# A packed attention with a gated convolution on one core: another hand-written order of issue for all five engines

## The chip, the core and the metric

The kernel runs on one core of a Trainium2 chip. Its engines are PE (TensorE: matrix products, with PEld for its weight loads), DVE (VectorE), ACT (ScalarE), POOL (GpSimd) and SP (SyncE, which here only issues DMA transfers). The metric is the time of one execution on the device in microseconds (us), as the median of several; shorter is better.

## The reference, cut to what matters

Eight batches of eight heads. In each head 32 packed queries `p` attend to 576 keys and values; the 32 results then serve as keys and values for the 576 real queries. The heads are laid side by side (512 columns), and a causal convolution of five taps over the 576 positions gives a gate for a value product, which an output product follows.

```python
def sm_attn(qq, kk, vv):
    s = scale * np.matmul(qq, kk.transpose(0, 1, 3, 2))
    s = s - np.max(s, axis=-1, keepdims=True)
    a = np.exp(s)
    a = a / (np.sum(a, axis=-1, keepdims=True) + 1e-09)
    return np.matmul(a, vv)
p_packed = sm_attn(p, k, v)              # 32 x 64 a head
out = sm_attn(q, p_packed, p_packed)     # 576 x 64 a head
...
for k in range(K):                       # K = 5
    gate_pre += conv_w[k][None, None, :] * xp[:, k:k + S, :]
gate = 1.0 / (1.0 + np.exp(-gate_pre))
val = x @ w_val
return (gate * val @ w_out).astype(np.float32)
```

## The kernel before, in words

The work is cut by batch into nineteen kinds of *streams*, Python generators that issue a few instructions and yield. A letter names the kind and a digit the batch, so `a3.2` means: take two more steps of batch 3's packed attention. The table `ORDER` at the top of the file lists such tokens one after the other, and `run` walks it. The class `InOrder` ties each instruction to the one before it on its engine, so each engine, and SP with its transfers, issues exactly in the order in which the table reaches it, and an instruction that has to wait holds up all that stands behind it on that engine. Tiles come from pools with few buffers (`NB`, `PSB`), and a load into a buffer waits until the last reader of its earlier content is done.

The streams that matter below:

- `K`, `V`, `Q`, `P`: loads of keys, values, queries (two transfers of 576 KB for a batch and tensor) and packed queries (four transfers of 64 KB for two batches), into `km`, `vm`, `qm`, `p`. `L`: loads of the weights (512 KB each), `wv_words` and `wo_words`, with `cw_words` between them.
- `W`, `C`, `O`: the weights come as 64-bit words and are turned into 32-bit numbers by ACT, DVE and POOL. `C` also spreads the convolution weights over the partitions with 40 small products (`spread`), which ACT copies into `cwb`.
- `k`, `q`: DVE transposes into `pT`, `kT` (two halves), `qT` (two halves).
- `a`: packed attention. Scores `s` (called `s1` here), row maximum `nb` on DVE, exponential `a` on ACT, then for each of two groups the transposes `at`, their copy `a1t` on ACT, the product with the values `pv`, and its two scaled copies into `ppd` on ACT.
- `p`: `ppTt`, the turned `ppd`, copied to `ppT` by ACT.
- `s`: scores of the real queries (also named `s`, called `s2` here), then transpose `t` and maximum `mx` on DVE, subtraction on POOL, exponential on ACT. `t`: sum `rs`, scaling on POOL, transpose `a` on DVE, split into high and low parts `a2h`, `a2l`.
- `w`: value weights folded with the packed result, `wp`, split into `wph` (ACT) and `wpl` (DVE).
- `x`: for batches 0 to 2 the convolution is folded into a product of 80 short matmuls for each half of the positions, with the weights `kx` (POOL, from `ppd` and `cwb`); for batches 3 to 7 it is a plain product, and `g` does the five taps on DVE.
- `v` (value product: `val`, then the gate on DVE, `gvh` on ACT, `gvl` on POOL) and `o` (output product `o`, copied by ACT to `osb` and stored).

On PE the groups `s`, `at`, `pv`, `x`, `wp` consist of many short matmuls (32 to 96 rows or columns); the groups `val` and `o` of twelve long ones (128 x 288 and 128 x 512). PSUM gives three two-bank buffers (`big`) for `s` (two each), `at`, `wp`, `x` (two each) and `val`, and one bank each for `pv`/`ppTt` and for `o`. All instructions are recorded under one line of the file, L84 before and L83 in the changed kernel (its table is one line shorter), so rows of the profile are told apart by their tiles.

Of the kernel before, what the change touches and what calls it, by code (L numbers as in the profile page):

```python
# [47 lines left out]
ON_POOL = {'al': (0, 1, 2), 'gvl': (0, 1, 2, 3, 4, 5, 6, 7)}  # L48

ORDER = """  # L50
L0 K0 W0.3 P0 K0 W0.2 L0 P0 W0.3 k0.3 W0.4 L0 a0 K1 W0.2 V0 W0.4 L0 W0.2 K1 a0.2 W0 a0.3 W0 a0 L0 k1 a0 C0.2 W0 k1
a0.2 k1 C0 a0.3 C0 W0.2 V0 a1 C0 W0 C0 a0 Q0 a1 q0 a0 Q0 q0 a1 W0 a0 L0 a1 p0 C0 p0 s0 O0.2 W0 a1 s0.6 P2 t0 P2 V1 C0
O0 a1 s0 C0.2 | V1 C0 a1.2 t0 a1 Q1 t0 s0 t0 a1.2 x0 t0 a1 w0 a1 t0 w0 t0 a1 k2 O0 t0.2 O0.3 Q1 K2 k2 a1 x0 K2 O0 w0
k2 a1 O0 x0 L0 t0 O0 x0 q1 O0 p1 x0 O0 x0 a2 O0.3 q1 a2 O0 x0 p1 a2.2 k3 V2 L0 v0.2 a2.2 K3 v0 a2 O0 K3 a2 s1 x1 a2 k3
O0 s1 a2 v0.2 s1.3 a2 s1.2 v0 t1 s1 t1 v0 k3 v0 a2 v0 a2 v0 V2 a2 t1 O0.2 a3 a2 s1 t1.3 v0 t1 a3 a2 P4 v0.2 a3.2 v0 t1
a3 p2 a3 O0 V3 a3 L0 a3 v0 w1 O0 w1 p2 P4 O0 V3 w1 v0 x1 O0.3 x1 Q2 x1 O0 t1 a3.3 t1 a3.2 q2 x1 K4 O0 a3 O0 v1 x1.2 Q2
k4 q2 O0.3 s2 v1 O0 Q3 O0 v1 a3 K4 O0 s2 v1.2 O0 s2 v1 q3 k4 o0 a3 Q3 s2 v1 s2 V4 s2 o0 s2 v1 Q4 t2 v1.2 s2 K5 v1 k4
t2 s2 o0 t2.5 v1 o0.2 v1 q3 a4 p3 a4.2 o0 K5 o0 v1 a4 p3 s3 o0 t2.2 o0 s3 x2 v1 a4 s3.4 o0.2 v1 a4.2 k5 x2 a4 t2 s3 a4
x2.2 a4 q4 w2.2 k5.2 x2 t3 a4 Q4 P6 w2 v2 P6 s3.2 t3 x2 K6 o0 t3 x2 v2 t3 a5 a4 t3 a4 V4 a5 x3 t3 o1 a5.2 K6 a4 a5 t3
v2 o1 a4 t3 a5 x3 t3 v2 k6 x3 V5 x3 v2 q4 a4 x3 t3 x3 p4 g3 o1 v2.2 k6 p4 v2 x3 Q5 V5 v2 g3 k6 o1 a5.2 v2 o1 g3.3 s4  # L60
v2 s4 a5 v2 K7 s4 o1 g3 q5 s4 g3 v2.2 a5 Q5 s4.2 g3 a5 s4 o1 a5 g3 t4 a5 a6 s4 w3 g3 a5 a6 o1 w3 a5 o1.2 a5 a6 v2 q5
g3 t4 w3 V6 g3 p5 Q6 g3 s4 t4 a6 v3 o1 g3 v3 o1 p5 t4 o1 a6 k7 v3 g3 v2 v3 s5 t4.2 g3 s5 o1 g3 s5 g3.2 t4 v3 s5 t4 s5
o1 t4 v3.2 o2 g3 s5 v3 o2 v3 g3 v3 o2 v3 g3.2 x4.4 o2 k7 x4 o2 v3 a6 x4 s5 q6 g4 a6 o2 g4 a6 g3 o2 Q6 x4 v3 g4 V6 a6
g4 t4 w4 s5 g4 o2 t5 a6 g4 v3 w4 a6.2 g4 w4 g4.3 o2 K7 o2 t5 a6 v4 o2 s5 v3 V7 g4 t5 g4.2 v4 t5 v3 o3 g4 t5 v4.2 t5.2
a6 o3 v4 a6 g4 v4 g4 v4 o3 a6 v4 g4 t5 q6 g4.2 Q7 g4.2 o2 v4 g4 v4 g4 o3 p6 x5.2 k7 o3 p6 t5 o3 x5 o3 v4 s6 o3 s6 g4
o3 x5 o3 s6 x5 s6.2 x5.2 o3 v4 s6.2 t5 v4 q7 a7 t6 o3 v4 s6 a7 g5 o3 g5 Q7 v4 a7 t6 a7 s6 t6 g5 a7 v4 o3 a7.2 w5 g5 a7
w5 g5.2 a7 t6 V7 g5 a7.3 w5 t6 a7 o3 g5.2 o4 a7 g5 a7 g5 v5 q7 a7 o4 v5 p7 g5 o4 g5 v5.2 o4 v5 g5.2 t6 g5 p7 v5.2 t6
v5 g5 o4 t6 v5 g5 s7 g5 v5 g5 o4 g5 s7 g5 t6 s7 o4 v5 o4 g5 x6 s7 x6.2 v5 x6 o4.2 g5 o4 s7.2 x6 t6 v5 x6 w6 t7 v5 g6.2
v5 x6 v5 w6 t7 g6 o5 g6 s7.2 g6 o5 g6 w6 o4 g6 t7 o5 s7 g6 o5.2 t7 o5 v6 g6 o5 g6 t7 g6.3 o5 v6 t7 v6.3 g6 t7 g6 v6 o5
v6.2 g6 o5 v6 o5 g6 t7 g6 v6 o5 g6.2 o5 v6 g6 o5 g6.2 x7.3 v6.2 g6 w7 v6 x7.2 t7.2 v6 w7 x7 v6 g7 o6 w7 o5 g7 o6 g7.3  # L70
o6 g7 v7.2 g7 o6 g7.2 o6 g7.2 v7 o6 x7 g7.2 v7 g7.2 v7.4 g7 o6.2 g7.3 v7.2 g7.4 v7.3 o7 g7 o7.2 v7.3 o7.2 o6 o7.14
o6.3
"""


# [632 lines left out]
```

## Time and profile before

| | |
|---|---|
| median of 3 runs | 288.07 us (287.93 to 290.36) |
| the profiled execution | 288.72 us, of which the profile's span is 286.9 us |
| PE busy | 257.1 us of the span (90%), 3676 matmuls |
| DVE busy | 236.1 us (82%) |
| ACT, POOL busy | 164.6 us (57%), 132.3 us (46%) |
| data | 33.57 MB read, 9.44 MB written |

Busy times are sums over an engine's own instructions; PE's ends are modelled. "PEclk" in the profile is the share of PE's full clock that was granted, in tenths. A wait that the profile can't put down to another engine or a transfer is called "issue". The chain of waits goes back from the last instruction to what released it, step by step.

### The profile page before, as it was taken

How to read it: one execution, taken by the hardware profiler on the slowest of the kernel's cores; microseconds unless marked ns; L12 is line 12 of the kernel's file. 1: busy time of each engine (PE TensorE's matmuls, PEld its weight loads, DVE VectorE, ACT ScalarE, POOL GpSimd, SP SyncE). 2: the span in 40 equal slices, each digit the busy share in tenths (PEclk: the TensorE clock that was granted, in tenths of full speed). 3: DMA queues.
4: the chain of work that ended last, by engine and by line, in shares of the span. 5: the costliest groups of instructions: out<-in, count | busy, mean ns of one | idle time of the engine just before them, and what ended most of it. 6: DMA issues, size and time to landing. Idle time of an engine off the chain costs nothing.

```text
span 286.9 us, 8501 instructions
## 1 busy us (share of the span) xinstructions
PE 257.1 (90%) x3676; PEld 191.0 (67%) x3676; DVE 236.1 (82%) x313; ACT 164.6 (57%) x306; POOL 132.3 (46%) x118
## 2 busy tenths in 40 slices
PE   0545789979899999999999999999999999999994
PEld 0143456667678766777677778766886688687863
DVE  2989489859969887899999989999998999787720
ACT  3372467729863558755847675758755465752421
POOL 1544286838778772324554317254074417401520
PEclk9997559979999999999999999999999999999999
DMA  7999953956594558783620664117111111110114
GB/s 264 318 318 292 329 206 89 279 135 181 204 324 131 197 158 220 198 238 125 200 79 37 203 202 121 73 59 220 39 39 53 57 39 73 40 53 21 39 43 177
DMA packets 25839, 43.56 MB, mean 152 GB/s; under 512 B 5829, under 2 KB 11973, under 8 KB 25802
## 3 DMA queue, kind: packets, MB, share of 16 engines
q1 hardware_dynamic: 25802, 43.02, 48.5%
q8 instruction: 29, 0.48, 0.7%
q14 instruction: 8, 0.07, 0.1%
HBM read 33.57 MB, written 9.44 MB: 150 GB/s over the span
## 4 chain that ended last, share of the span: by engine, by line
PE 66%; DVE 18%; ACT 6%; issue 4%; DMA 2%; POOL 1%; SPq 1%; ACTq 0%; DVEq 0%
PE o L84 26%; PE val L84 13%; DVE sig L84 10%; PE s L84 8%; PE x L84 7%; PE pv L84 5%; PE at L84 4%; DMA wv_words<-in_moe_w_val_dram 2%; PE wp L84 2%; ACT sig L84 1%; PE ppTt L84 1%; ACT a L84 1%; SPq L84 1%; PE spread L84 1%; DVE a2l L84 1%
## 5 line engine op out<-in xcount | busy, mean ns | idle before, releaser
L84 POOL TENSOR_TENSOR gvl<-sig,gvh 128x576 fp32r<-128x576 f32 x32 | 51.3, 1604 | 64.7 <-ACT gvh L84 64.5
L84 DVE SCALAR_TENSOR_TENSOR sig<-xp,cw,sig 128x576 f32<-128x576 f32 x80 | 71.1, 888 | 3.2 <-ACT sig L84 1.8
L84 PE MATMUL o<-woh,gvh 128*128 128x512 f32 x144 | 58.9, 409 | 2.3 <-ACT osb L84 1.6
L84 PE MATMUL o<-woh,gvl 128*128 128x512 f32 x144 | 56.9, 395 | 0.0
L84 PE MATMUL o<-wol,gvh 128*128 128x512 f32 x144 | 56.7, 394 | 0.0
L84 PE MATMUL val<-a2h,wph 128*128 128x288 f32 x128 | 39.9, 312 | 0.0
L84 PE MATMUL val<-a2h,wpl 128*128 128x288 f32 x128 | 38.5, 301 | 0.0
L84 PE MATMUL val<-a2l,wph 128*128 128x288 f32 x128 | 38.2, 299 | 0.0
L84 PEld LDWEIGHTS o<-woh,gvh 128*128 128x128 f32 x144 | 27.0, 188 | 13.7 <-ACT osb L84 3.6
L84 ACT CAST gvh<-sig 128x576 fp32r<-128x576 f32 x32 | 21.6, 674 | 25.3 <-DVE sig L84 25.2
L84 DVE SCALAR_TENSOR_TENSOR sig<-sig,val 128x576 f32<-128x576 f32 x32 | 23.7, 740 | 10.5 <-PE val L84 7.0
L84 PEld LDWEIGHTS o<-woh,gvl 128*128 128x128 f32 x144 | 27.1, 188 | 6.8 <-POOL gvl L84 0.5
L84 ACT ACTIVATE osb<-o 128x512 f32<-128x512 f32 x34 | 20.3, 596 | 17.8 <-PE o L84 14.8
L84 PEld LDWEIGHTS o<-wol,gvh 128*128 128x128 f32 x144 | 27.1, 188 | 5.0
L84 POOL TENSOR_TENSOR t<-t,mx 128x576 f32<-128x576 f32 x16 | 20.1, 1254 | 21.8 <-DVE mx L84 21.8
L84 POOL TENSOR_TENSOR t<-t,rs 128x576 f32<-128x576 f32 x16 | 21.9, 1368 | 17.4 <-DVE rs L84 17.3
L84 PEld LDWEIGHTS val<-a2h,wph 128*128 128x128 f32 x128 | 24.6, 192 | 5.2 <-issue 2.0
L84 PEld LDWEIGHTS val<-a2h,wpl 128*128 128x128 f32 x128 | 24.6, 192 | 0.8 <-DVE wpl L84 0.3
L84 PEld LDWEIGHTS val<-a2l,wph 128*128 128x128 f32 x128 | 24.6, 192 | 0.0
L84 ACT ACTIVATE sig<-sig 128x576 f32<-128x576 f32 x20 | 13.7, 685 | 19.0 <-DVE sig L84 18.9
L84 PE MATMUL s<-kT,pT 32*32 32x288 f32 x512 | 16.0, 461 | 9.5 <-DVE kT L84 9.3
L84 PEld LDWEIGHTS pv<-vm,a1t 96*32 96x32 f32 x768 | 13.3, 119 | 13.9 <-issue 6.1
(80 smaller groups left out, 455.6 us busy)
## 6 DMA issues: line engine op xcount, KB each, us to landing
km<-in_k_dram SPq DMA_DIRECT2D x16, 576.0 KB, 5.9
vm<-in_v_dram SPq DMA_DIRECT2D x16, 576.0 KB, 6.9
qm<-in_q_dram SPq DMA_DIRECT2D x16, 576.0 KB, 6.8
out_dram<-osb SPq DMA_DIRECT2D x36, 256.0 KB, 2.1
wv_words<-in_moe_w_val_dram SPq DMA_DIRECT2D x4, 512.0 KB, 6.1
wo_words<-in_moe_w_out_dram SPq DMA_DIRECT2D x4, 512.0 KB, 8.3
p<-in_p_dram SPq DMA_DIRECT2D x16, 64.0 KB, 4.1
cw_words<-in_moe_conv_w_dram SPq DMA_DIRECT2D x1, 20.0 KB
```

The lines of the kernel that those rows point to most:

```text
L84: made = getattr(self.engine, op)(*args, **kw)
```

## The change

Only the string `ORDER` differs: the same tokens in another sequence, so the same instructions, tiles and transfers, in another order on each engine. No size, buffer count or operation changes. Nearly every line of the table is different; the start reads:

```diff
-L0 K0 W0.3 P0 K0 W0.2 L0 P0 W0.3 k0.3 W0.4 L0 a0 K1 W0.2 V0 W0.4 L0 W0.2 K1 a0.2 W0 a0.3 W0 a0 L0 k1 a0 C0.2 W0 k1
...
+L0 W0.6 L0 K0 W0 P0 K0 W0.2 P0 k0.3 W0.4 a0 L0 V0 a0 W0.3 k1 W0.3 L0 W0.2 L0 W0 a0.2 K1 k1 a0.4 W0 a0 C0 a0 W0 a0.2 C0
...
```

**PE.** The groups of matmuls stand in the same order in both kernels from the first instruction up to and with the scores `s2` of batch 2 (the 39th group), and again from the third value group of batch 5 to the end. Between them, groups move by one to five places. The place where most moves: from the first value group of batch 1 (`val_0`) to the fourth output group of batches 0 and 1 (`o_3`). One row, the first, stands for each group; `s_2` is `s2` of batch 2, `s_4` is `s1` of batch 4, `s_3` is `s2` of batch 3, `ppTt` is that of batch 3. Before:

```order
L84 MATMUL val_0_1258<-a2h_892,wph_1073 128x288
L84 MATMUL s_2_0_1287<-qT_0_1184,ppT_1076 32x288 x2
L84 MATMUL val_1_1333<-a2h_892,wph_1073 128x288
L84 MATMUL o_0_1353<-woh,gvh 128x512
L84 MATMUL val_2_1387<-a2h_892,wph_1073 128x288
L84 MATMUL o_1_1417<-woh,gvh 128x512
L84 MATMUL val_3_1432<-a2h_892,wph_1073 128x288
L84 MATMUL s_4_0_1448<-kT_0_1351,pT_1277 32x288 x2
L84 MATMUL ppTt_1482<-ident,ppd_1044 128x128 x3
L84 MATMUL o_2_1493<-woh,gvh 128x512
L84 MATMUL s_3_0_1514<-qT_0_1349,ppT_1509 32x288 x2
L84 MATMUL o_3_1563<-woh,gvh 128x512
```

In the changed kernel:

```order
L83 MATMUL val_0_1263<-a2h_912,wph_1073 128x288
L83 MATMUL s_2_0_1286<-qT_0_1132,ppT_1035 32x288 x2
L83 MATMUL ppTt_1345<-ident,ppd_1046 128x128 x3
L83 MATMUL val_1_1351<-a2h_912,wph_1073 128x288
L83 MATMUL o_0_1364<-woh,gvh 128x512
L83 MATMUL s_4_0_1387<-kT_0_1329,pT_1327 32x288 x2
L83 MATMUL o_1_1427<-woh,gvh 128x512
L83 MATMUL val_2_1464<-a2h_912,wph_1073 128x288
L83 MATMUL o_2_1482<-woh,gvh 128x512
L83 MATMUL s_3_0_1500<-qT_0_1440,ppT_1442 32x288 x2
L83 MATMUL val_3_1551<-a2h_912,wph_1073 128x288
L83 MATMUL o_3_1568<-woh,gvh 128x512
```

`s_4` now stands ahead of `o_1`, `val_2` and `val_3`, so two value or output groups stand between `s_2` and `s_4` where five stood, and three between `s_4` and `s_3` where one stood; `ppTt` of batch 3 goes five groups ahead. Further on the same is done on a smaller scale: an output and a value group come between the transposes and the `pv` of batch 4, and in batch 7 two value groups come ahead of the second `pv`.

**ACT, from the second `pv` of batch 0 to the first `ppd` of batch 1.** `a_1_0` and `a_1_1` are batch 1's exponentials, `t_0` batch 0's, `ppd` the copies after `pv`. Before:

```order
L84 ACTIVATE ppd_178<-pv_1_292,sm_0_113 128x64
L84 ACTIVATE a_1_0_328,sm_1_254<-s_1_0_255,nb_1_0_319 128x576
L84 ACTIVATE ppd_178<-pv_1_292,sm_0_113 128x2x64
L84 COPY ppT_341<-ppTt_336 128x384
L84 ACTIVATE wo_top<-wo_words 128x512
L84 ACTIVATE wo_words<-wo_words 128x512
L84 ACTIVATE a_1_1_384,sm_1_254<-s_1_1_256,nb_1_1_334 128x576
L84 ACTIVATE t_0_343<-t_0_343 128x18x32
L84 ACTIVATE p_392<-p_392 128x512
L84 COPY cwb<-spread 128x640
L84 COPY a1t_0_467<-at_0_468 96x768
L84 ACTIVATE t_0_343<-t_0_343 128x18x32
```

In the changed kernel:

```order
L83 ACTIVATE ppd_182<-pv_1_289,sm_0_112 128x64
L83 ACTIVATE ppd_182<-pv_1_289,sm_0_112 128x2x64
L83 ACTIVATE a_1_0_334,sm_1_253<-s_1_0_254,nb_1_0_324 128x576
L83 COPY ppT_342<-ppTt_328 128x384
L83 ACTIVATE a_1_1_381,sm_1_253<-s_1_1_255,nb_1_1_340 128x576
L83 ACTIVATE wo_top<-wo_words 128x512
L83 ACTIVATE t_0_344<-t_0_344 128x18x32
L83 ACTIVATE wo_words<-wo_words 128x512
L83 COPY a1t_0_455<-at_0_456 96x768
L83 ACTIVATE t_0_344<-t_0_344 128x18x32
L83 COPY cwb<-spread 128x640
L83 ACTIVATE ppd_454<-pv_0_480,sm_1_253 128x64
```

Both copies into `ppd` now come ahead of the exponential `a_1_0`, and the copy into `cwb` now stands behind the copy `a1t_0` and the second exponential of `t_0`; the scaling of `p` has left this stretch.

**SP, the loads of batches 2 to 4.** Both pieces begin with `vm_0` of batch 2. `km_0` and `km_1` are batch 3's, the first `vm_1` is batch 2's, the second `vm_0` and `vm_1` batch 3's, `qm` is batch 2's; `wo_words` are the third and the fourth quarter of the output weights. Before:

```order
L84 DMA vm_0_756<-in_v_dram 96x4x384
L84 DMA wo_words<-in_moe_w_out_dram 128x1024
L84 DMA km_0_778<-in_k_dram 128x2x576
L84 DMA km_1_797<-in_k_dram 128x2x576
L84 DMA vm_1_931<-in_v_dram 96x4x384
L84 DMA p_1008<-in_p_dram 32x8x64 x4
L84 DMA vm_0_1042<-in_v_dram 96x4x384
L84 DMA wo_words<-in_moe_w_out_dram 128x1024
L84 DMA vm_1_1080<-in_v_dram 96x4x384
L84 DMA qm_0_1135<-in_q_dram 128x2x576
```

In the changed kernel:

```order
L83 DMA vm_0_749<-in_v_dram 96x4x384
L83 DMA km_0_776<-in_k_dram 128x2x576
L83 DMA wo_words<-in_moe_w_out_dram 128x1024
L83 DMA vm_1_885<-in_v_dram 96x4x384
L83 DMA km_1_907<-in_k_dram 128x2x576
L83 DMA wo_words<-in_moe_w_out_dram 128x1024
L83 DMA p_1041<-in_p_dram 32x8x64 x4
L83 DMA qm_0_1078<-in_q_dram 128x2x576
L83 DMA vm_0_1081<-in_v_dram 96x4x384
L83 DMA qm_1_1084<-in_q_dram 128x2x576
```

`km_0` has moved ahead of the third `wo_words`, `km_1` behind `vm_1`; the four transfers of `p` now come behind the fourth `wo_words`, and both halves of batch 2's `qm` have come forward, ahead of batch 3's values.

**DVE, ahead of `wpl` of batch 1.** The first step on the fourth pair of output weights (`wo_words`, one TENSOR_SCALAR) now stands directly behind the maxima `nb` of batch 3, where before it stood three steps ahead of `wpl`, behind the transpose `a` of batch 1. The transpose `a` itself now stands behind `sm` of batch 3. The second step (SCALAR_TENSOR_TENSOR) stands where it stood.

More of the change, by code (lines that the diff above doesn't have):

```diff
@@ L50 @@
 ORDER = """
-L0 K0 W0.3 P0 K0 W0.2 L0 P0 W0.3 k0.3 W0.4 L0 a0 K1 W0.2 V0 W0.4 L0 W0.2 K1 a0.2 W0 a0.3 W0 a0 L0 k1 a0 C0.2 W0 k1
[L52 to L70, printed above, removed]
@@ L71 @@
-o6 g7 v7.2 g7 o6 g7.2 o6 g7.2 v7 o6 x7 g7.2 v7 g7.2 v7.4 g7 o6.2 g7.3 v7.2 g7.4 v7.3 o7 g7 o7.2 v7.3 o7.2 o6 o7.14
-o6.3
+L0 W0.6 L0 K0 W0 P0 K0 W0.2 P0 k0.3 W0.4 a0 L0 V0 a0 W0.3 k1 W0.3 L0 W0.2 L0 W0 a0.2 K1 k1 a0.4 W0 a0 C0 a0 W0 a0.2 C0
+K1 a0 k1 C0 V0 C0 a1 W0 a0.2 C0 W0 Q0.2 a0 q0 a1 q0 p0 W0.2 a1 L0 C0.2 a1 p0 s0 a1 O0 C0 s0 C0 s0.5 a1 O0 s0 C0 | t0
+a1.2 t0 P2 s0 C0 V1 a1.3 O0 x0 L0 t0.4 a1 t0 a1 w0 V1 w0 O0 t0 P2 O0 K2 a1 O0.2 k2 a1.2 w0 x0 k2 O0 Q1 K2 Q1 x0 p1
+x0.2 t0 k2 q1 O0 q1 x1 O0.2 t0 x0.2 p1 O0.4 a2 V2 O0 a2.2 v0 a2 k3 a2 v0 K3 a2.3 s1 O0.2 a2 v0 k3 s1 a2 v0 s1 L0 s1 a2
@@ new lines @@
+s1 v0 V2 s1.2 v0 s1 a2 O0 K3 v0 t1 a2 O0 s1 t1 L0 v0 k3 v0.2 a2 t1.3 a2.2 t1 a3.2 v0 a3 t1 a3 v0 a3 O0 v0 p2.2 v0 a3
+t1 P4 a3 O0 a3 v0 w1.2 O0 w1 Q2 v0 V3 O0 Q2 x1 q2 O0.2 a3 x1 a3 x1 a3.3 t1 P4 x1 q2 O0.2 t1 O0 V3 x1 a3.2 v1 O0.2 K4
+x1 O0 s2 K4 v1 O0.2 a3 O0 k4.2 O0 Q3 s2.2 K5 k4 s2.2 v1 s2 v1 p3 Q3 v1 o0 t2 o0 v1 a4 o0 a4.2 v1 o0 q3 p3 o0 V4 q3 o0
+t2 v1 s2 Q4 t2 s2 t2 a4 t2 a4 v1.2 s2 v1 k5 o0 t2 s3 P6 o0 a4 v1 t2 K5 s3 x2 t2 v1 P6 v1 o0 v1 o0 s3.2 t2 s3 a4 s3 o0
+a4 v1 x2 V4 k5 x2.2 k5 a4 t2 a4 q4 w2.2 s3 K6 x2.2 t3 x2 w2 v2 s3 a4 v2 s3 Q4 a5 t3.3 a5 t3 a4 o1 t3 a5.2 t3 x3 k6 a4
@@ new lines @@
+a5 o1 k6 v2 t3 v2.2 K6 v2 a4 v2 x3 V5 v2 x3 v2 x3 o1 k6 x3 a4 t3 o0 V5 o1 v2 x3 a4 a5 q4 g3.2 x3 p4 g3 p4 g3 t3 g3 o1
+a5.2 Q5 s4 v2 g3 s4 q5 a5 Q5 a5.2 g3 s4 o1 a5 g3 K7 v2 s4 V6 v2.2 o1 s4 v2 a5 s4 w3.2 g3 a5 s4 o1 a5 g3 t4 a5 g3 s4
+g3.2 w3 a6 p5 o1 a6 t4.2 a6 t4 p5 a6 o1 v2 v3 g3 s4 g3 o1 a6 g3 q5 o1 v3 o1 v3.2 s5 g3.2 t4.2 g3 v3 g3 t4 o1 s5 V6 o1
+v3.3 o2 t4 s5.2 o2 s5.2 g3 v3.3 g3.2 x4.2 o2 x4 Q6 o2 k7 x4.2 s5 o2 x4 o2 k7 a6 v3 g3 g4 q6 s5 g4 t4 Q7 a6 o2 g4 t4 x4
+g4.2 v3 a6 o2 g4 w4 v3 g4 t5 o2 w4 g4 t5 a6.3 w4 a6.2 o2 a6 g4.2 v4 o2 g4 t5 v3 o2 s5 v3 g4 v4 o3 Q6 t5.2 a6 g4 a6 v4
@@ new lines @@
+K7 g4 o3 v4 g4 t5 g4 v4.2 t5 g4 v4 g4 v4 t5 g4 v4 q6 o3 g4.2 v4 o3 g4.2 p6 x5 t5 o3 x5.2 o3.2 p6 V7 k7 o3 s6.2 o3 v4
+g4 x5 v4 s6 o3 s6 x5 s6.2 x5 v4 x5 q7 t5 t6 o3 g5 a7 t6 v4 s6 v4 a7.3 v4 o3 a7 t6 g5 Q7 o3 a7 o3 g5 a7 w5 a7 w5 g5 t6
+g5 V7 g5.2 a7.3 w5 t6 g5.2 s6 a7 g5 o4 g5 a7 q7 o4 g5 v5.2 g5 v5 g5 o3 v5 o4 v5 s6 a7.2 o4 g5 t6 a7 g5 v5 p7.2 v5 o4
+t6 v5 g5.2 t6 v5 o4 g5 s7 v5 g5 o4 g5 t6 s7 g5 v5 g5 x6 o4 x6 s7 x6.2 s7.2 o4 s7.2 o4 x6 g5 x6 s7 o4 v5 t6 v5 w6 g6 t7
+v5.3 w6 g6.2 t7 o4 g6 o5 g6 x6 t7 w6 o5 g6 o5.2 g6 t7 g6.2 t7 v6 s7 o5.3 g6.4 v6 o5 v6 o5 t7 v6 g6 t7 g6 v6 o5 v6.3
@@ L73 @@
+g6.2 v6 o5 t7 g6.2 v6 g6 t7 g6 o5.2 g6.2 v6 x7.2 v6 o5 x7 t7 g6 v6.2 w7 x7 o5 v6 w7.2 x7 v6 x7 g7.2 o6 g7.3 o6.2 g7 v7
+o6 g7 o6 v7 g7 x7 v7 g7.3 v7 g7.3 v7 g7 o6.2 v7.2 o6 g7 v7 g7.2 v7 g7 v7 g7.4 v7 o6 v7 g7 v7.2 o7.3 v7.2 o7.16 o6.3
 """
```

## The prediction

> **What bounds the kernel now.** I read the slices first, then a table of stretches, then PE's waits.
>
> ```profile
> span 286.9 us, 8501 instructions
> PE 257.1 (90%) x3676; PEld 191.0 (67%) x3676; DVE 236.1 (82%) x313; ACT 164.6 (57%) x306; POOL 132.3 (46%) x118
> PEclk9997559979999999999999999999999999999999
> DMA  7999953956594558783620664117111111110114
> ```
>
> A slice is 7.2 us. PE's granted clock falls to half in the fourth to sixth and dips again in the ninth; the transfers are at their limit in nearly the first six slices, and are light from the 25th on. The table by stretch (busy time and count for PE, PEld, DVE, ACT, POOL, then PE's clock, DMA share, GB/s) says where PE could still gain:
>
> ```profile
> 25.50:42.60 17.10, 12.44 (x266) 8.01 (x265) 11.55 (x19) 8.86 (x18) 9.13 (x9) 0.50 0.85 253
> 59.70:63.10 3.40, 3.40 (x31) 3.13 (x19) 0.76 (x2) 1.15 (x3) 1.71 (x2) 0.50 0.47 113
> 63.10:80.00 16.90, 16.02 (x401) 11.97 (x399) 15.70 (x22) 14.24 (x29) 12.63 (x10) 1.00 0.67 200
> 80.00:187.00 107.00, 107.00 (x1597) 81.21 (x1593) 95.54 (x129) 66.05 (x127) 50.59 (x48) 1.00 0.55 166
> ```
>
> From 80 to 187 us PE is busy in 107.00 of 107.00 us at full clock. Nothing is to be had there, however the groups are spaced, unless PE's own work shrinks, and that is the same 3676 matmuls. What PE loses, it loses ahead of 80 us, and after 223 us, where DVE leads. So a new order gains by what it does to the first 80 us, and loses by any wait that it brings into the full stretch. PE's waits up to 80 us (total, times, longest) that are not the mere start-up:
>
> ```profile
> PE pv L84 <- issue: 3.7, 2, 2.0
> PE spread L84 <- issue: 1.5, 1, 1.5
> PE at L84 <- DVE wpl L84: 0.9, 1, 0.9
> ```
>
> Three stops of 5.2 us are put down to nothing but "issue". I take them for PE waiting for its own program:
>
> ```profile
> q8 instruction: 29, 0.48, 0.7%
> q8 instruction: 1, 0.02, 5.6%
> 59.13 1.04 PE L84 MATMUL pv<-vm,a1t 96*32 96x64 f32 x43 [1.69 <-issue]
> ```
>
> The first row is the whole span: 29 fetches in 0.48 MB, 16.5 KB each, for 3676 matmuls and as many weight loads: one fetch for about 253 instructions, or 127 matmuls. The second is the window from 56.4 to 57.8 us alone: one fetch lies there, none in the 4.9 us ahead, and `pv` of batch 2 stops after five of its 48 matmuls until 59.13. So a fetch that starts about 56.5 serves PE by 59.1. Why it starts late, SP's issues show:
>
> ```profile
> 47.83 0.34 SPq L84 DMA_DIRECT2D wo_words<-in_moe_w_out_dram  x1
> 48.27 2.43 SPq L84 DMA_DIRECT2D km<-in_k_dram  x2
> 50.79 0.42 SPq L84 DMA_DIRECT2D vm<-in_v_dram  x1
> ```
>
> These four transfers are 512 and three times 576 KB, 2.3 MB, and the fetch begins when they are through. I read it as a queue: the fetch stands behind the loads issued ahead of its request. The Trainium skill (Runtime: NRT & Kernel Launch, "Instruction fetch mechanics") has programs refilled in blocks of 256 instructions, ahead of time and "mostly hidden"; the count agrees, and 26 of the 29 fetches cost PE no marked stop, but three did. By that rule alone this wait could not change, and the third term below would be 0.
>
> **The change part by part.** PE's order is the same through the first 39 groups, up to `s2` of batch 2, which ends at 84.3 us in this trace. All three stops lie ahead of that and fall on the same matmuls as now. The spacing itself, on PE, therefore touches only the full stretch and is worth 0 there by the row of 107.00. What can act early are the other engines' new orders. The sum is made against the profiled execution, 288.72 us.
>
> *Term 1, the start of batch 0 and `cwb`: +0.25 us.*
>
> ```profile
> 27.07 0.73 ACT L84 ACTIVATE a<-s,nb 128x576 f32<-128x576 f32 x1
> 37.02 0.69 ACT L84 COPY cwb<-spread 128x640 f32<-128x640 f32 x1 [0.71 <-PE spread L84]
> 38.60 0.68 ACT L84 ACTIVATE t<-t 128x576 f32<-128x576 f32 x1
> 38.16 1.54 POOL L84 TENSOR_TENSOR kx<-ppd,cwb 128x640 f32<-128x640 f32 x1
> 43.66 2.55 PE x L84 x67
> 104.92 2.59 PE x L84 x80
> ```
>
> ACT's exponential `a` no longer stands between the two `ppd` copies: `ppTt` and `s2` of batch 0 come 0.7 us sooner. But `cwb` now follows the second exponential of `t`, which ends at 39.28: it starts 39.3 - 0.7 = 38.6, ends 39.3, and `kx` starts there instead of at 38.16, 1.1 us late. POOL's next steps and DVE's last transpose follow `kx` in order and release `x` of batch 0, so `x` starts 1.1 us late. It has something to give back: now its first half takes 3.40 us (43.66 to 47.06), with a break after 67 matmuls, against 2.59 for the same 80 at 104.92, 0.8 us. Starting later, its block of program has come. 1.1 - 0.8 = +0.25, rounded; bounds -0.5 (the 0.7 kept) and +1.2 (nothing given back).
>
> *Term 2, `wpl` of batch 1: -0.9 us.*
>
> ```profile
> L84 DVE TENSOR_SCALAR wo_words<-wo_words 128x512 uint32<-128x512 uint32 x4 | 2.3, 586 | 0.5 <-ACT wo_top L84 0.5
> 77.21 2.97 PE x L84 x79
> ```
>
> One `wo_words` step of 0.59 us leaves the way to `wpl`, for which PE waits 0.9 us: -0.6. The `x` behind it takes 2.97 against 2.59, 0.4 us that I count as a fetch just late; in the new order three loads stand ahead of it instead of four (`qm` of batch 2 has gone forward), so 0.3 comes back. Bounds 0 and -1.3, the whole of both.
>
> *Term 3, the stop at 57.4 us: -1.5 us.*
>
> ```profile
> 60.17 3.12 PE val L84 x12
> 64.04 1.78 PE val L84 x12
> ```
>
> `km` of batch 3 now goes ahead of `wo_words` and no longer waits for its buffer; it waits only for DVE's `kT` of batch 2. So 576 KB of the 2.3 MB can pass up to 1.4 us sooner (at the 0.4 MB in a us that the busy slices carry), and the fetch with it. The stop of 1.69 falls to something between 0.3 and 1.69; I take 0.9, a gain of 0.8. The stop also costs clock: the stretch at 0.50 follows it, and twelve `val` take 3.12 us in it against 1.78, 1.34 us. The 0.9 us wait at 76 us brought no fall of the clock, 1.69 did; a stop of 0.9 is on the edge, and I count half, 0.7. Bounds 0 and -3.0, both gone. The skill's page on the clock (TensorE: Matmul & The Clock Gate, "What's actually happening") asks for an idle window of about 3.4 us before the clock falls; by that the 1.34 would not hang on this stop and the term would be -0.8. Here 1.69 us of idle were enough, so the row decides.
>
> *Term 4, new meetings in the full stretch: +0.9 us.*
>
> ```profile
> L84 DVE STREAM_TRANSPOSE kT<-km 128x1152 f32<-128x1152 f32 x16 | 21.4, 1351 | 0.0
> L84 DVE STREAM_TRANSPOSE t<-s 128x576 f32<-128x576 f32 x16 | 12.4, 773 | 7.4 <-PE s L84 7.4
> L84 DVE TENSOR_REDUCE mx<-t 128x18 f32<-128x576 f32 x16 | 11.9, 747 | 0.3
> 82.77 1.54 PE s L84 x63
> 84.31 1.79 PE val L84 x12
> 86.10 2.80 PE o L84 x12
> ```
>
> `s1` of batch 4 now comes right behind `ppTt`, one `val` and one `o`: at 84.31 + 0.3 + 1.8 + 2.8 = 89.2. Its PSUM buffers come free and its keys are there when DVE has done, after `s2` of batch 2 (84.31) at the soonest, with `kT` still at work: one `kT` started beforehand and ending some 0.9 us into it, then `t`, `mx`, the other `kT`, `t`: 84.31 + 0.9 + 0.77 + 0.75 + 1.35 + 0.77 = 88.9. That just meets. DVE is busy in 95.54 of the 107 us, so it has little to catch up with. There are some three such places (also `ppTt` of batch 5, moved ahead by two groups, and the output groups behind it, whose buffer ACT now empties after three more steps). For each the nearest row is the 0.9 us wait for `wpl`; I take 0.3 each, bounds 0 and +2.
>
> After 210 us PE's order is the same again, and DVE, which leads there, has the same work ahead of each `val`: 0, within 0.5 either way.
>
> **The sum:** 0.25 - 0.9 - 1.5 + 0.9 = -1.25, 288.72 to 287.5 for an execution like the profiled one. That one lies 0.65 above the median of the runs, so 288.07 - 1.25 = **286.8 us**. With these terms' own doubts 285.3 to 288.8.
>
> **The rivals.** *A, the program comes in time throughout.* Both the stop at 57.4 and the clock it costs go (-3.0), term 2 goes whole (-1.3), the middle costs nothing: 288.07 - 4.3 = 283.8. For it: the 2.3 MB are the only load ahead of that fetch. Against it: `kT` now stands behind `wpl` on DVE, so `km` may start later than I take it.
>
> *B, slower: the same stop, moved into the full stretch.* From `at` of batch 4 to `at` behind `s1` of batch 5 PE has over 300 short matmuls, almost in one piece in both orders, and needs a fetch in the middle:
>
> ```profile
> q8 instruction: 1, 0.02, 4.9%
> ```
>
> This is the window 108.3 to 109.5 us. It has come in time. In the new order `qm` of batch 4 and both halves of `km` of batch 6 are issued ahead of it, where before the first half of `km` was the only one: two more transfers, 2.9 us at the same rate. If less than about 0.4 us of slack is there now, PE stops. The price is that of the stop at 57.4, 1.69 + 1.34 = 3.0, with the gains of terms 2 and 3 at a third (-0.8) and the middle at its +0.9: 288.07 + 0.25 + 3.0 + 0.9 - 0.8 = 291.4. Against it: that fetch has spare time that no row shows, and other loads have been spread out.
>
> *C, nothing moves.* The loads shift by as much as the requests, the three stops stay: 288.1.
>
> **How the numbers follow.** A measurement of this kernel tells about 1% from no change, 2.9 us. The forecast has a chance of 0.32, C 0.15, A 0.30, B 0.23. A lies beyond the 1%, B just beyond, the forecast and C within. So faster 0.30, same 0.47, slower 0.23. The range reaches towards A and B as far as the bounds go: the lower ends add to -0.5 - 1.3 - 3.0 = -4.8 and the upper to +3.2; I cut both a little, 283.6 to 291.2.
>
> **What would show it.** Right: the "issue" stops at `pv` of batch 0 and at `spread` stay near 2 and 1.5 us; that at `pv` of batch 2 is under 1 us; `x` of batch 0 starts later; the stretch from 80 to 187 us is full but for waits under 1 us. A shows in no half clock after 45 us. B shows in an "issue" stop and half clock between 105 and 120 us. The forecast is wrong if the stretch from 80 to 187 loses over 2 us to ACT or DVE, or if the start up to 40 us moves by over 1 us: nothing above counts on that.

## The result, and the profile after

The changed kernel takes 291.69 us in the median (290.33 to 293.07, six runs) beside 288.0 us of the kernel before on the same chip: a ratio of 1.0143, with an interval of 1.0108 to 1.0177. Ratios, here and below, are taken from the runs within 1.5% of the fastest of their kernel. It is slower by 3.7 us and lies half a microsecond above the predicted range. Its profiled execution took 290.33 us, the shortest of the six, and that of before 288.72, a long one of its kernel; so the two traces differ by 1.6 us where the medians differ by 3.7.

The slices of the changed kernel's page:

```profile
span 288.6 us, 8500 instructions
PE 257.0 (89%) x3676; PEld 190.8 (66%) x3676; DVE 235.7 (82%) x313; ACT 164.1 (57%) x306; POOL 131.7 (46%) x118
PEclk9999558999999999999999999999999999999999
DMA  7999973979617888088143516238101011100014
```

PE has the same work (257.0 and 257.1 us). The half clock comes half a slice later and its second dip is gone. The full stretch, by stretches (PE, PEld, DVE, ACT, POOL, PE's clock, DMA share, GB/s):

```profile
80.00:187.00 107.00, 105.87 (x1541) 80.45 (x1530) 94.56 (x128) 63.67 (x122) 50.34 (x44) 1.00 0.50 153
112.00:114.10 2.10, 1.11 (x17) 0.24 (x12) 0.24 (x1) 0.00 (x0) 0.00 (x0) 1.00 1.01 224
```

PE is no longer busy all of it. 1.13 of the 107 us are lost, and 0.99 of those lie in the two microseconds of the second row, in which the transfers are at their limit and DVE, ACT and POOL have next to nothing to do. PE's waits, first two rows of before that the prediction doesn't show, then those of the changed kernel (total, times, longest):

```profile
PE s L84 <- DVE kT L84: 9.3, 1, 9.3
PE ppTt L84 <- ACT ppd L84: 1.4, 1, 1.4
```

```profile
PE s L83 <- DVE kT L83: 12.4, 1, 12.4
PE pv L83 <- issue: 2.4, 2, 1.2
PE spread L83 <- issue: 1.8, 1, 1.8
PE x L83 <- issue: 1.6, 2, 1.0
PE ppTt L83 <- ACT ppd L83: 0.7, 1, 0.7
PE at L83 <- DVE wpl L83: 0.3, 1, 0.3
```

Two rows are clearly worse. The first scores start at 12.45 us instead of 9.29, so 3.2 us are lost before PE has done anything. And `x`, which had no marked stop, now has two for nothing but "issue". Three rows are better, in the direction forecast: the stops of `pv` (3.7 before), the wait for `ppd` (1.4) and that for `wpl` (0.9). Of the 1.3 us that `pv` gains, 0.8 are in batch 0, where the prediction expected no change. In these two traces PE is 3.2 us late at the first scores, 2.1 at the first `val` of batch 0 (55.01 against 52.93), 0.5 early at the `at` behind `wpl` (75.92 against 76.39) and 0.5 late at `s2` of batch 2 (83.29 against 82.77). So by 83 us this one execution had made most of its late start good.

Where the first 3.2 us go stands in the first rows of SP and ACT (start, duration). Before, then changed:

```profile
0.74 0.36 SPq L84 DMA_DIRECT2D wv_words<-in_moe_w_val_dram  x1
1.63 1.94 SPq L84 DMA_DIRECT2D p<-in_p_dram  x4
6.87 0.63 ACT L84 ACTIVATE p<-p 128x512 f32<-128x512 f32 x1 [1.61 <-DMA p<-in_p_dram]
```

```profile
0.74 0.85 SPq L83 DMA_DIRECT2D wv_words<-in_moe_w_val_dram  x2
2.11 2.06 SPq L83 DMA_DIRECT2D p<-in_p_dram  x4
10.03 0.63 ACT L83 ACTIVATE p<-p 128x512 f32<-128x512 f32 x1 [3.40 <-DMA p<-in_p_dram]
```

The first change of the table, `L0 W0.6 L0 K0` for `L0 K0 W0.3`, puts a second 512 KB of weights ahead of batch 0's keys and packed queries. SP issues `p` half a microsecond later; its data come 3.2 us later, and ACT, DVE's transposes and PE follow. The stop in `x` of batch 2 in the chain of the changed kernel, and the loads that SP issued ahead of it:

```profile
109.86 2.57 PE x L83 x68
112.43 0.99 issue
113.42 0.73 PE x L83 x12
```

```profile
105.34 0.37 SPq L83 DMA_DIRECT2D km<-in_k_dram  x1
105.76 0.46 SPq L83 DMA_DIRECT2D qm<-in_q_dram  x1
106.60 0.37 SPq L83 DMA_DIRECT2D km<-in_k_dram  x1
108.90 0.33 SPq L83 DMA_DIRECT2D vm<-in_v_dram  x1
```

The queues in the window 107.0 to 110.9 us, then in 110.9 to 112.0:

```profile
q1 hardware_dynamic: 624, 1.37, 95.3%
...
q1 hardware_dynamic: 216, 0.42, 98.7%
q8 instruction: 1, 0.02, 5.7%
```

In the first window only data move, 1.37 MB of them with the queues 95% full; PE's program block is read in the second. In the trace of before that fetch lay in the window that begins at 108.3.

### The profile page after: what moved, and what is told of

The parts are those of the page before. It is cut to its first block, busy times and chain, and to the rows that moved or that the text cites. A ratio compares the mean times of both kernels' runs of the same rounds, so it can differ in the third digit from the quotient of the medians.

```text
span 288.6 us, 8500 instructions
## 1 busy us (share of the span) xinstructions
PE 257.0 (89%) x3676; PEld 190.8 (66%) x3676; DVE 235.7 (82%) x313; ACT 164.1 (57%) x306; POOL 131.7 (46%) x118
## 4 chain that ended last, share of the span: by engine, by line
PE 66%; DVE 20%; ACT 5%; issue 4%; DMA 2%; SPq 1%; POOL 1%; ACTq 0%; DVEq 0%
PE o L83 26%; DVE sig L83 13%; PE val L83 11%; PE s L83 9%; PE x L83 7%; PE pv L83 5%; PE at L83 3%; PE wp L83 2%; DMA p<-in_p_dram 2%; ACT sig L83 2%; DVE rs L83 1%; PE ppTt L83 1%; SPq L83 1%; PE spread L83 1%; DVE kT L83 1%
## 5 line engine op out<-in xcount | busy, mean ns | idle before, releaser
L83 POOL TENSOR_TENSOR gvl<-sig,gvh 128x576 fp32r<-128x576 f32 x32 | 49.9, 1561 | 66.7 <-ACT gvh L83 64.7
L83 DVE SCALAR_TENSOR_TENSOR sig<-xp,cw,sig 128x576 f32<-128x576 f32 x80 | 72.6, 907 | 3.1 <-ACT sig L83 1.6
L83 PE MATMUL val<-a2h,wph 128*128 128x288 f32 x128 | 39.2, 306 | 0.0
L83 PE MATMUL val<-a2h,wpl 128*128 128x288 f32 x128 | 37.9, 296 | 0.2 <-DVE wpl L83 0.2
L83 PEld LDWEIGHTS val<-a2h,wph 128*128 128x128 f32 x128 | 24.0, 188 | 5.0 <-issue 1.3
```

The lines of the kernel that those rows point to most:

```text
L83: made = getattr(self.engine, op)(*args, **kw)
```

## The experiments

All kernels compute the whole of the reference; they differ in the table alone. Each ratio is to the kernel before on the same chip, with its interval. Theory F says that the loss is made by program fetches that stand behind loads, theory H that it is the late start.

**1. The start alone, from both sides.** `after_head` gives the changed kernel the start of the kernel before:

```diff
-L0 W0.6 L0 K0 W0 P0 K0 W0.2 P0 k0.3 W0.4 a0 ...
+L0 K0 W0.3 P0 K0 W0.2 L0 P0 W0.3 k0.3 W0.4 L0 a0 ...
```

> The changed kernel with the start of the kernel before up to the first scores (keys and packed queries of batch 0 ahead of the second weights again). First scores near 9.3 us instead of 12.45 by both theories. Theory F (the loss is made by PE's program fetches that stand behind loads, in x of batches 1 and 2; the late start is made good by 63 us): the median stays near 291.7, at most 0.7 lower. Theory H (the late start of 3.2 us is what costs, in most executions): 288.5 to 289.2.

Measured 1.0036 (1.0004 to 1.0069), where the changed kernel has 1.0143 (1.0108 to 1.0177): the start is worth 1.1%, 3.1 us. On this point Theory F, which had it made good by 63 us, fell. `before_head` does the reverse, the same lines with the signs exchanged:

> The kernel before with the start of the changed kernel alone, up to the first scores: two weight loads ahead of batch 0's keys and packed queries, and their conversion ahead on ACT and DVE. If the late start is carried to the end by itself: first scores at 11 to 12.5 us instead of 9.3, ratio 1.007 to 1.012. If it is made good within the first 63 us by stops that shrink: 0.998 to 1.003.

Measured 1.0103 (1.0033 to 1.0173). The kernel before loses 3.0 us (1.0 to 5.0) with nothing but this start, and its first scores come 2.2 us later than the 9.3 of before:

```profile
PE s L84 <- DVE kT L84: 11.5, 1, 11.5
```

**2. Which part of the start.** `after_p` moves the four small transfers of `p` alone ahead of the second weights:

```diff
-wv_words x2, km_0, p x4, km_1
+wv_words, p x4, wv_words, km_0, km_1
```

> The changed kernel with the four small transfers of batch 0's packed queries directly behind the first weight load, ahead of the second; all else as in the changed kernel. If the late packed queries alone make the first scores late: they start at 9.5 to 10.5 us instead of 11 to 12.5, and the time falls by 1.5 to 3 us (ratio 1.004 to 1.009). If the keys, which still stand behind two weight loads, are as late: first scores stay above 11 us, ratio 1.012 to 1.015.

Measured 1.0157 (1.0088 to 1.0227): no gain that can be seen. In its trace `p` waits on ACT until 8.70 us, behind the conversion of the second weights, and the second half of the keys holds DVE until 11.57; the first scores come at 11.2. `after_k0` puts all of the loads back, and leaves the conversion of the second weights where the change put it:

```diff
-L0 W0.6 L0 K0 W0 P0 K0 W0.2 P0 k0.3
+L0 K0 P0 K0 L0 W0.9 P0 k0.3
```

> The changed kernel with the keys and packed queries of batch 0 ahead of the second weight load again, but the conversion of the second weights still ahead of p on ACT. If the transfers alone make the late start: first scores at 9.3 to 10.3 us, ratio 1.003 to 1.007. If ACT's order keeps it (p cannot be scaled until the second weights, which now land later, are converted): first scores at 11.5 to 14 us, ratio 1.011 or more.

Measured 1.0177 (1.0129 to 1.0225), with the first scores at 13.2 us, later than with the change whole. ACT's rows, and the first of DVE behind them, show why:

```profile
9.67 0.66 ACT L83 ACTIVATE wv_top<-wv_words 128x512 f32<-128x512 f32 x1 [4.34 <-DMA wv_words<-in_moe_w_val_dram]
10.78 0.61 ACT L83 ACTIVATE p<-p 128x512 f32<-128x512 f32 x1
...
11.42 0.45 DVE L83 STREAM_TRANSPOSE pT<-p 128x256 f32<-128x256 f32 x1 [5.00 <-ACT p L83]
```

No transfer holds `p` up any more, but it stands behind a conversion that now waits for its own load. Loads and conversion must move together: each alone brought nothing that can be seen, both together 1.1%. The start is a matter of what waits in order on SP *and* on ACT.

**3. Early part and late part.** `early_new` is the changed kernel up to the scores `s2` of batch 2 and the kernel before from there; `late_new` is the reverse.

```diff
 steps up to s2 of batch 2:  early_new: changed   late_new: before
 the steps left over:        early_new: before    late_new: changed
```

> The order of the changed kernel up to the scores s2 of batch 2, then that of the kernel before. Theory F: the start is absorbed and the stop at 111 us is gone: 288.0 to 288.8. Theory H: near 291.

Measured 1.0100 (1.0065 to 1.0134).

> The order of the kernel before up to the scores s2 of batch 2, then that of the changed kernel, with its wider spacing. Theory F: the stop in x of batch 2 near 110 us comes with the new load order: 289.5 to 290. Theory H: 288.0, as before.

Measured 1.0104 (1.0064 to 1.0145). Each half costs 1%; together that is 2.0% where the whole has 1.4, and the intervals, 0.35 to 0.4% each way, leave open how much of it they share. The early half costs what its start costs by itself (1.0103, known to 0.7%). What else is in it, the forecast's first three terms, is taken up again below with two more pairs of kernels. In the late half the stop in `x` of batch 2 is there, 4.24 us from its first matmul to the next group, where `early_new`, with before's loads, has 2.61.

**4. The stop in x of batch 2.** `after_k6` moves one load:

```diff
 qm_1 of batch 4
-km_1 of batch 6
 vm_0 of batch 5
+km_1 of batch 6
```

> The changed kernel with one load moved on SP: the second half of km of batch 6 behind the first half of vm of batch 5, so that it is issued behind the request for the program and not ahead of it. Theory F: the fetch that now begins at 110.95 begins by 109.6, the second x of batch 2 takes 2.6 us instead of 4.3 and the median falls by 1.7 to 290.0. Theory H, or a stop that has another cause (buffers, the weights kx): x keeps its stop and the time stays at 291.7.

Measured 1.0083 (1.0045 to 1.0121), but its trace says that the fetch still began at 110.8 and that `x` still took 3.82, with a stop of 0.52 instead of 0.99: a miss for the expectation. The load that I moved had been issued at 106.60; it may hardly have stood ahead of the request, whose time no trace shows. `after_mid` moves `qm` of batch 4 too:

```diff
-qm_1 of batch 4
-km_1 of batch 6
 vm_0 of batch 5
+qm_1 of batch 4
+km_1 of batch 6
```

> The changed kernel with two loads moved on SP: the second half of qm of batch 4 and the second half of km of batch 6 behind the first half of vm of batch 5, so that only the first half of km of batch 6 is issued in the 3 us ahead of the program fetch of PE that is needed near 112 us. Theory F (the fetch waits for the loads issued ahead of its request): the fetch begins 1.4 us sooner than with qm there, the second x of batch 2 takes 2.6 to 2.9 us instead of 3.8 to 4.3, and the time falls by 1.4 to 1.7 us against the changed kernel (ratio to the kernel before near 1.009). Rival (the stop belongs to the new order on PE itself, whatever the loads): x keeps 3.8 us or more, ratio 1.014.

Measured 1.0091 (1.0058 to 1.0125). Its chain, its SP rows, and the queue of the window 109.5 to 110.5 us:

```profile
110.67 2.61 PE x L83 x80
```

```profile
106.14 0.37 SPq L83 DMA_DIRECT2D km<-in_k_dram  x1
109.71 0.32 SPq L83 DMA_DIRECT2D vm<-in_v_dram  x1
110.08 0.79 SPq L83 DMA_DIRECT2D qm<-in_q_dram  x1
```

```profile
q8 instruction: 1, 0.02, 5.9%
```

With one load ahead of it instead of two, the fetch came ahead of 110.5 although PE was 0.8 us later than in the changed kernel, and `x` took its 80 matmuls without a stop. With the changed kernel's loads the second `x` took 4.29, 3.98, 4.24 and 4.37 us (the changed kernel, `after_head`, `late_new`, `after_k0`), and in `after_p` 4.99, with a stop of 1.69 and half clock from 119.0 to 122.4. With `qm` moved it took 2.61 in all four kernels that have it. PE's order is the same in all of these, so the stop is the fetch's and not the spacing's. In time the move is worth 0.5% here, with intervals that overlap, and 0.8% and 1.2% in the two pairs below, with intervals that don't. That `after_k6`, which keeps a stop, measures as well as `after_mid` (1.0083 and 1.0091) isn't explained.

**5. The two undone together, and the spacing by itself.** `after_head_mid` has the start of before and the two loads moved:

> The same two loads moved, and the start of the kernel before. If the late start (about 1.07% by the run that undid it) and the stop in x (0.5%) are two separate losses that add: ratio to the kernel before 0.997 to 1.000. If they share a cause, or the wider spacing itself costs: 1.004 to 1.007.

Measured 0.9960 (0.9922 to 0.9998): the two losses add, and with both undone the new order is level with the old or a little ahead. `late_mid` is `late_new` with the two loads moved, so that nothing is left of the change but the spacing on PE and the order that goes with it on the other engines:

> The order of the kernel before up to the scores s2 of batch 2, then that of the changed kernel with its wider spacing, and the two loads moved. With the stop in x gone only the spacing is left. If spacing is worth nothing on a full PE: ratio 1.000 to 1.004. If the spacing itself costs: 1.010 as without the moved loads.

Measured 0.9986 (0.9954 to 1.0018). The full stretch in its trace:

```profile
88.00:196.00 108.00, 107.87 (x1559) 81.55 (x1561) 98.52 (x132) 66.64 (x125) 50.59 (x46) 1.00 0.51 159
```

107.87 of 108 us: the spacing itself neither gains nor costs more than the 0.3% of the interval.

**6. The stop at 57 us, which the prediction counted as a gain.** `before_p4` is the kernel before with `p` of batches 4 and 5, which has to wait until 54.7 us, ahead of two loads:

```diff
-km_1 of batch 3
-vm_1 of batch 2
 p of batches 4 and 5
+km_1 of batch 3
+vm_1 of batch 2
```

> The kernel before with one step moved on SP: the packed queries p of batches 4 and 5, which wait for a buffer until 54.7 us, ahead of the second half of km of batch 3 and the second half of vm of batch 2. These two loads, 1.15 MB, then go out behind the request for the program that PE needs at 57.4 us. Theory F: that fetch begins near 53 us instead of 56.5, the stop of 1.7 us in pv of batch 2 goes, and with it the half clock in the val behind it where it falls: 1.5 to 3.0 us less than before. Rival (the stop has another cause, or km and vm come too late for s and pv near 66 us): same as before or up to 1 us more.

Measured 1.0085 (1.0052 to 1.0118): slower. The stop in `pv` went as Theory F has it, but `vm` came late, and PE waited there instead:

```profile
66.87 1.51 PE L84 MATMUL pv<-vm,a1t 96*32 96x64 f32 x48 [4.66 <-DMA vm<-in_v_dram]
```

`before_v2` leaves `vm` in its place and moves `km` alone:

```diff
-km_1 of batch 3
 vm_1 of batch 2
 p of batches 4 and 5
+km_1 of batch 3
```

> The kernel before with only the second half of km of batch 3 moved behind the packed queries p of batches 4 and 5; the second half of vm of batch 2, whose delay cost 4.7 us in the run with both moved, goes ahead of p at its old place in time. 576 KB less stand ahead of the fetch that PE needs at 57.4 us: it begins near 55 us instead of 56.5, the stop of 1.7 us falls below 0.4, the clock stays whole behind it, km arrives before its transpose at 65 us. Theory F: 1.4 to 3.0 us faster than before, ratio 0.990 to 0.995. Rival (the gain is given back by a later fetch or load, as in the run with both moved): 0.998 or more.

Measured 1.0024 (0.9995 to 1.0054). The rival held: the stop fell to a third of a microsecond, and eight microseconds later the moved load is itself late.

```profile
57.67 0.86 PE L84 MATMUL pv<-vm,a1t 96*32 96x64 f32 x43 [0.33 <-issue]
...
64.67 1.38 DVE L84 STREAM_TRANSPOSE kT<-km 128x1152 f32<-128x1152 f32 x1 [2.32 <-DMA km<-in_k_dram]
...
66.11 1.47 PE L84 MATMUL s<-kT,pT 32*32 32x288 f32 x48 [1.76 <-DVE kT L84]
```

`before_wo` moves a load that can wait, the third quarter of the output weights:

```diff
-wo_words (third quarter)
 km_0, km_1 of batch 3
 vm_1 of batch 2
 p of batches 4 and 5
+wo_words (third quarter)
```

> The kernel before with the third quarter of the output weights, which nothing uses before 65 us, moved behind the packed queries p of batches 4 and 5; km of batch 3 and vm of batch 2 stay ahead and in time. Theory F (the stop at 57.4 us is time that can be had if the load moved is one that can wait): the fetch begins near 55 us instead of 56.5, the stop falls below 0.5, the clock stays whole, no wait for km or vm takes its place; 1.7 to 3.0 us less than before, ratio 0.990 to 0.995. Rival (whatever is gained here is lost again ahead of the full stretch, at a load or another fetch): 0.998 or more, as with km moved.

Measured 0.9978 (0.9945 to 1.0010), a smaller gain than Theory F expected and not to be told from the rival's 0.998, though its trace has no stop in that `pv` at all, no wait in its place, and a span of 283.6 us, 3.3 less than the profiled execution of before. `head_mid_wo`, the same on top of `after_head_mid`:

> The changed kernel with the start of the kernel before, the two loads near 106 us moved, and the third quarter of the output weights moved likewise behind p. Theory F: 0.987 to 0.993 of the kernel before, below both kernels. Rival: 0.996, as without the last move.

Measured 0.9982 (0.9949 to 1.0015): no gain over 0.9960 either. Its profiled execution, the longest of its twelve runs, has no stop in that `pv`, but a new one in `x` of batch 1, some 20 us later, where the program block began to come only at 76.9:

```profile
PE x L83 <- issue: 1.8, 1, 1.8
```

In this execution PE lost at a later fetch what it had saved, as the rival has it. What delayed that fetch wasn't tested.

**7. More executions of the two kernels.** The changed kernel again:

> The changed kernel once more, beside the others: ratio 1.011 to 1.018 as first measured. First scores between 11 and 12.5 us, a stop of 1.2 to 1.7 us in the second x of batch 2.

Measured 1.0137 (1.0057 to 1.0217), the first scores at 12.9 us, a little later than expected, 3.96 us for that `x`, 1.35 more than without a stop. And the kernel before, unchanged, since the short span of `before_wo` and its median don't fit together:

> The kernel before once more, for a second look at the stop near 57 us. If the stop of 1.7 us and the half clock behind it belong to every execution: both are there again, span near 286.9. If they come and go with the start and the phase of the clock: a stop between 0.5 and 2 us, the half clock only in some, span 284 to 288.

> The kernel before, a third look. If the stop near 57 us and the half clock behind it belong to every execution: both are there, span near 286.9. If they come and go: the half clock only in some, span 284 to 288.

The one took 285.01 us with a span of 283.2, the other 289.38 with 287.6. The chain around `pv` of batch 2 in the one, and in the other:

```profile
56.94 0.33 issue
57.27 0.86 PE pv L84 x43
58.13 1.78 PE val L84 x12
```

```profile
57.49 2.80 issue
60.29 0.86 PE pv L84 x43
61.15 2.96 PE val L84 x12
```

The stop belongs to some executions and not to others: 0.33, 1.69 and 2.80 us in three traces of one kernel. In the short execution the fetch began at 54.5 us, ahead of `p`; in the long one at 57.5, behind it. The loads ahead were issued half a microsecond later in the long one, which may be what decides which of the two is first; no run tests that. 3.7 of the 4.4 us between the two spans lie there: 2.5 of stop and 1.2 of clock, in twelve `val` of 2.96 instead of 1.78. So the stop and the half clock come and go, as the second of the two theories has it, by more than it allowed: the 0.33 us and the span of 283.2 lie below its ranges.

## Why the prediction was wrong

**The step that failed is one that isn't there.** The sum begins with the start of batch 0 and `cwb`, at 27 us. The prediction said that it would be wrong "if the start up to 40 us moves by over 1 us: nothing above counts on that", and that happened. SP's new order from its first row on, two `wv_words` ahead of `km` and `p`, was not looked at: I read SP from batch 2 on. The price could have been read off: 512 KB more ahead of what the chain's first link waits for, 1.3 us at the rate of the busy slices as a floor. In the traces of kernels with this start the first scores came at 11.1 to 12.9 us, in those with the old one at 9.3 to 9.9. Measured by itself it is 1.0% of before, 3.0 us (1.0 to 5.0), and 1.1 and 1.3% in the two pairs that undo it (the changed kernel and `after_head`, `after_mid` and `after_head_mid`). That alone turns the forecast of -1.25 into a loss.

**PE's early order** is indeed the same, and the spacing is worth nothing on a full PE, as said: 0.9986 for `late_mid`.

**Term 1, +0.25.** The part on `ppd` came as worked out: PE's wait at `ppTt` is 1.4 us in every trace with the old early order and 0.7 in every one with the new. The other part didn't: with the old start, `cwb` went at 36.87 in `after_head`, not at 38.6, and `x` of batch 0 began at 41.9 there and at 43.5 in `after_head_mid`, against 42.8 to 44.3 in the three traces of before, not 1.1 us late.

**Term 2, -0.9.** The wait for `wpl` fell from 0.9 to 0.3, the 0.6 forecast. The `x` behind it took 3.9 us in the changed kernel's first trace and 3.0 in its second, so the 0.3 expected there didn't come.

**Term 3, -1.5.** The stop fell from 1.69 to 1.16 and the clock stayed whole in the first trace of the changed kernel; in the second the stop was 1.71, with the half clock. Over all traces it isn't smaller: 1.16 to 1.98 us in the nine with the new order of these loads, 1.7 in the mean, and 0.33 to 2.80 in the six with the old one, 1.5; half clock followed in six of the nine and in three of the six. So the term took one execution's stop for the kernel's, and that the fetch comes sooner when `km` goes first isn't borne out.

The stop in `spread`, which was to stay near 1.5 us, grew: it is 1.2 to 4.3 us in the ten traces with the new early order, 2.8 in the mean, and 1.0 to 1.8 in the eight with the old start and the old early order, 1.5. No experiment changes that stop alone.

Terms 1 to 3 together, forecast at -2.15 us or 0.75%, can be read from three pairs of kernels that differ in the rest of the early part alone: 0.0% (`early_new` and `before_head`), -0.7% (`after_head` and `late_new`) and -0.3% (`after_head_mid` and `late_mid`), each known to 0.5 to 0.8%. So they are a gain of between nothing and what was forecast, and not enough to pay for the start.

**Term 4, +0.9.** None of those waits came. `s1` of batch 4, which I put at 89.2, stands at 89.68 in the chain directly behind `o`, with PE 0.5 us late already, and beside the fetch 0.14 us are lost in the full stretch. It measures next to 0.

**Rival B** was right in place, cause and sign and was given 0.23. The fetch for `x` of batch 2 stood behind `qm` of batch 4 and `km` of batch 6, and began at 110.95 instead of 108.44, 2.5 us later, where 2.9 were worked out; PE itself was 0.5 us late. The price was 1.7 us of `x` instead of 3.0, since a stop of 0.99 us brought no half clock. What spoke against it, "spare time that no row shows", came to about a microsecond (2.0 us later against PE, 0.99 of stop) and was not enough. The time that B gives, 291.4, is near the 291.69 measured by chance: it has a clock in it that didn't fall, and lacks the start. The stated range, which ends at 291.2, leaves out this rival of the prediction's own.

So the change's two halves each lose 1%, by things that have nothing to do with its spacing: the order of the first loads with the work on ACT that goes with it, and two loads that stand ahead of one program block. The experiments have 1.0 to 1.3% for the start and 0.5 to 1.2% for the loads, 1.5 to 2.5% in all; the 1.4% measured lies just below that, which leaves room for the small gain of the early part. What stays open: how that gain divides among its terms, and what makes the spread of one kernel's runs. Those of `before_wo`, without the stop in the one trace, still lie between 285.3 and 290.3 us.

## What to carry to other kernels

Read each queue from its first row when an order changes: what stands ahead of the first link of the chain had to be paid for here (in `before_head` 2.2 us at the first scores and about 3 us of time), on every queue that the link passes, SP and ACT. Before a wait that one profile shows is counted as a gain, look at more executions of the same kernel: a wait that depends on which of two transfers is first can be 0.3 us in one and 2.8 in the next. And when loads are moved into a stretch where PE is full, ask which program block is fetched there: a load that nothing needs for 15 us can stop PE within seven.

## What the runs showed of the hardware

Behind a stop in `pv` of batch 2 the clock fell or didn't, with a sharp edge in the stop's length. In the 16 profiled executions where PE stops there for "issue", 0.33, 0.33, 0.61, 1.15, 1.16, 1.36 and 1.66 us left the clock whole; 1.69, 1.70, 1.71, 1.71, 1.92, 1.92, 1.98, 2.51 and 2.80 us were followed by a stretch of 3.41 us at 0.50. With the wait of 4.66 us for `vm` in `before_p4` the stretch was 6.83 us, twice that, and began at 64.2, inside the wait. The edge lies near half of the 3.41 us. The Trainium skill (TensorE: Matmul & The Clock Gate, "What's actually happening") asks for an idle window of about 3.4 us; the stretches agree with that length, but here 1.69 us without work were enough.

The clock changes in steps of that length. In each of the 19 traces the times within the span at which it changes lie whole multiples of 3.41 us apart: 25.53, 42.60, 59.67 and 63.08 in that of before. So the half clock began between 0.1 and 1.8 us behind the end of the stop, and what it cost hung on what fell into its 3.41 us: the twelve `val` behind the stop took 3.12 us in one execution and 2.41 in another. No run has a long stop that lies across the end of such a step, so whether that would leave the clock whole is open.

The fetch of a program block waits for the loads that were issued ahead of it. In the seven traces with `qm` of batch 4 and the first half of `km` of batch 6 issued some 5 us ahead, the fetch for the second `x` of batch 2 began 0.6 to 1.8 us behind the first matmul of that `x`; in the four with `qm` moved it began 0.5 to 1.2 us ahead of it. In all seven PE went on 2.3 to 2.5 us after the fetch began. When the block was asked for no trace shows; the waiting is read from this comparison. The Trainium skill (Runtime: NRT & Kernel Launch, "Instruction fetch mechanics") calls this fetching mostly hidden. Here it was hidden only where little was queued ahead of it.
